# An mLSTM and SoLU kernel: the first product in float16 parts, x turned by a transfer, and a fixed order of operations

## The chip, the cores and the metric

The kernel runs on one core of one Trainium2 chip. The metric is the device time of one execution in microseconds; the value before is the median of 3 runs. The core has a matrix engine (TensorE, PE in the profile; its weight loads are listed as PEld), VectorE (DVE), ScalarE (ACT), GpSimd (POOL) and SyncE (SP), whose queue issues the transfers here. Tiles lie in SBUF; the results of matrix products lie in PSUM, where the kernel keeps eight banks of 128 x 512 float32 values.

## The reference

4 batches, 8 heads, 768 steps, head size 40. For each batch and head a recurrence with gates runs over the steps; its outputs, gated and laid side by side (8 x 40 = 320), are the rows x of a block with d_ff = 1024.

```
for t in range(768):                       # attention part, per batch and head
    m_new  = max(f[t] + m, i[t])
    f_stab = exp(f[t] + m - m_new);  i_stab = exp(i[t] - m_new);  m = m_new
    C = f_stab * C + i_stab * outer(v[t], k[t])
    n = f_stab * n + i_stab * k[t]
    y[t] = sigmoid(o[t]) * (C @ q[t]) / max(abs(n . q[t]), 1)

h    = x @ w_in                            # 3072 x 320 by 320 x 1024
sm   = exp(h - max(h)) / (sum(exp(h - max(h))) + 1e-9)
solu = h * sm
ln   = (solu - mean(solu)) / sqrt(var(solu) + 1e-6) * g_ln
out  = ln @ w_out                          # 3072 x 1024 by 1024 x 320
```

w_in and w_out come as 64-bit floats; the kernel decodes them from their bits.

## The kernel before, in words

**Units.** The steps are cut into 6 chunks of 128, and a unit is one chunk of one batch with all 8 heads: 24 units, chunk by chunk over the batches. For a unit, `unit(u)` sets down these operations.

*Attention.* Transfers on SP's queue bring v and k (`tk`), q and k turned (`qk`), the running gate sums spread over all partitions (`gb`) and, for four units at a time, the output gates (`sg`). ACT makes the decay factors `d` (L990, 8 exponentials of 128 x 128). PE makes the scores `ps` (L1034, into two banks), DVE multiplies them with `d` into `p` (L1047). PE adds up y in a third bank: the inter step `yx` (L1074, old state times q, only for chunks after the first) and two intra steps `yi` (L1101, p times v). DVE normalises (L1117 to L1136), POOL applies the output gate (L1148): that is x. The state step `sx` (L1159) gives this chunk's part of the state, which DVE adds to the decayed state (L1186, or L1188 for the first chunk).

*First product.* PE turns x (L1200, three transposes into a bank), ACT rounds it to the parts `xh` (L1206, L1205) and DVE takes the rest `xl` (L1211, L1217), both in the format float32r. w_in is split alike, as soon as each of its five pieces has been decoded (L675 to L710, then L748 to L777). Of the four part products three are formed: 8 terms, each in two halves of 512 columns, so 16 matmuls a unit (L1245) into one of two double banks `ph`.

*The rest.* DVE takes the row maximum (L1260), ACT the exponential (L1267), DVE h times it (L1282), ACT the squares (L1292) and a float16 rounding (L1306), POOL its remainder (L1310). A transposing transfer turns both float16 parts (L1319). The second product is 24 float16 matmuls of 320 columns (L1378) into the single bank `so_`, ACT scales the result out (L1394, with a factor that POOL's power, L1357, gives) and SP stores it.

**Banks.** `sy` is a ring of three banks for scores, y, the state step's result and the turned x; `ph` has two double banks, `so_` one.

**The order.** Each engine executes its instructions in the order in which they stand, and that order is written out before the program is built. `Plan.find` plays through all operations with the durations and priorities given in the code (`RANK`, `NUDGE`) and lists them in the order of their planned starts; `Plan.run` emits them in this list's order. PE operations with a `mix` number are split into steps (four products, or six matmuls of the second product), and an attention step that is ready together with a step of the first or second product is joined to it: their matmuls are emitted in turn. While PE would be idle at the start, `find` puts in idle matmuls (L1413; each is two passes, 51 of them here), whose results nobody reads. The w_out scale uses L822. Only these few matmuls read float32 in two passes: the attention products, L822 and L1413. The select matrix L498 copies one broadcast column with two operations of a POOL instruction.

## Time and profile before

| | |
|---|---|
| median of 3 runs | 317.56 us (316.15 to 318.75) |
| the profiled execution | 317.33 us, of which its span 315.6 us |
| granted TensorE clock | 0.998 |
| busy: PE, PEld, DVE, ACT, POOL | 297.6, 252.4, 209.4, 202.0, 154.7 us |
| transfers on SP's queue | 59.13 MB, 70.5% of 16 engines' span |

A row of the groups names the line, the engine, the operation, the tiles out<-in and the shape, then `xcount | busy us, mean ns of one | idle us of the engine just before them, and what ended most of it`. A row of the waits reads: engine and line, what it waited for, microseconds in total, times, longest. A row of the chain in order of time has start, duration and what ran; the chain follows back from the last instruction to what released each step, so on PE a piece's duration is what it moved the chain by, not how long the matmul was in the array. A row of the stretches has the stretch, its length, the busy time (and number) of PE, PEld, DVE, ACT and POOL, the clock, the share of the transfer engines and GB/s. In the transfers' row the last number is the median time from issue to landing in us.

### The profile page before, as it was taken

The page shows a single profiled execution, that of the slowest core. Times are in us where ns is not written, and L with a number is a line of the kernel's source. Part 1 is how long each engine was busy: PE and PEld are TensorE (multiplying, and loading weights), DVE is VectorE, ACT ScalarE, POOL GpSimd, SP SyncE. Part 2 cuts the span into 40 slices and gives each one's busy share as a digit, 9 for nine tenths or more (in the row PEclk, how much of TensorE's full clock was granted, in tenths as well). Part 3 has the DMA queues.
Part 4 walks back from the last instruction along what each step waited for, and adds up shares of the span by engine and source line. Part 5 has one row for each costly group of instructions (what it writes and reads, how often), then busy time and mean ns, then how long its engine had stood idle before and what let it go on. Part 6 is the DMA issues. An engine that isn't in the chain of part 4 may idle for free.

```text
span 315.6 us, 6358 instructions
## 1 busy us (share of the span) xinstructions
PE 297.6 (94%) x2255; PEld 252.4 (80%) x2255; DVE 209.4 (66%) x548; ACT 202.0 (64%) x433; POOL 154.7 (49%) x159
## 2 busy tenths in 40 slices
PE   0499999999999999999999999999999999999984
PEld 0398978889778888898889888888988888788753
DVE  5965958999857375766868477764675666574530
ACT  2367669698776866786847678744894754452441
POOL 7165276686685536673672544756334504431300
PEclk9999999999999999999999999999999999999999
DMA  7799937955499955997499754999675534244351
GB/s 230 260 329 393 391 110 247 223 205 86 127 230 247 295 180 82 329 218 226 137 206 281 201 162 115 258 255 259 189 197 150 132 72 58 53 93 84 71 125 43
DMA packets 70255, 59.53 MB, mean 189 GB/s; under 512 B 52944, under 2 KB 59280, under 8 KB 70224
## 3 DMA queue, kind: packets, MB, share of 16 engines
q1 hardware_dynamic: 70224, 59.13, 70.5%
q8 instruction: 18, 0.29, 0.4%
q14 instruction: 13, 0.11, 0.1%
HBM read 42.50 MB, written 4.03 MB: 147 GB/s over the span
## 4 chain that ended last, share of the span: by engine, by line
PE 93%; DVE 4%; issue 1%; DMA 1%; ACT 1%; SPq 0%; ACTq 0%; DVEq 0%
PE ph L1245 31%; PE sy L1101 10%; PE sy L1034 8%; PE sy L1159 5%; PE sy L1074 5%; PE so__163 L1413 4%; PE sy L1200 3%; PE so__404 L822 2%; PE so__1923 L1378 1%; PE so__3758 L1378 1%; PE so__3786 L1378 1%; PE so__3713 L1378 1%; PE so__1761 L1378 1%; PE so__1521 L1378 1%; PE so__2638 L1378 1%
## 5 line engine op out<-in xcount | busy, mean ns | idle before, releaser
L1378 PEld LDWEIGHTS <-big 128*128 128x128 f16 x576 | 62.1, 114 | 17.6 <-issue 5.0
L1101 PEld LDWEIGHTS sy<-tk,p 128*128 128x128 f32 x384 | 63.5, 191 | 6.0 <-DVE p L1047 0.6
L990 ACT ACTIVATE d<-gb,bG 128x128 f32<-128x128 f32 x192 | 60.5, 392 | 6.7 <-DVE p L1047 3.1
L1310 POOL TENSOR_TENSOR us<-e,us 128x1024 f16<-128x1024 f32 x23 | 49.2, 2140 | 29.2 <-ACT us L1306 22.6
L1101 PE MATMUL sy<-tk,p 128*128 128x41 f32 x384 | 56.8, 245 | 0.4 <-DVE p L1047 0.4
L1267 ACT ACTIVATE e<-ph,nm 128x1024 f32<-128x1024 f32 x24 | 26.7, 1112 | 28.0 <-DVE nm L1260 27.8
L1047 DVE TENSOR_TENSOR p<-sy,d 128x512 f32<-128x512 f32 x48 | 31.2, 684 | 18.7 <-PE sy L1034 11.7
L1260 DVE TENSOR_REDUCE nm<-ph 128x1 f32<-128x1024 f32 x24 | 29.3, 1222 | 17.3 <-PE ph L1245 17.1
L1245 PE MATMUL ph<-wih,xh 128*128 128x512 f32 x96 | 40.0, 464 | 0.0
L1148 POOL TENSOR_TENSOR x<-x,sg 128x320 f32<-128x320 f32 x24 | 21.3, 887 | 33.7 <-DVE x L1136 23.0
L1245 PE MATMUL ph<-wil,xh 128*128 128x512 f32 x96 | 37.1, 435 | 0.0
L1282 DVE SCALAR_TENSOR_TENSOR e<-ph,s,e 128x1024 f32<-128x1024 f32 x24 | 30.6, 1276 | 4.0 <-ACT e L1267 3.2
L975 POOL TENSOR_SCALAR_AFFINE_SELECT gb<-gb 128x1024 f32<-128x1024 f32 x24 | 27.1, 1130 | 11.1 <-DMA gb<-gd 11.1
L1292 ACT ACTIVATE sq<-e,a 128x1024 bf16<-128x1024 f32 x24 | 27.6, 1149 | 5.3 <-DVE e L1282 4.4
L1245 PE MATMUL ph<-wih,xl 128*128 128x512 f32 x96 | 30.6, 419 | 0.0
L1034 PEld LDWEIGHTS sy<-qk 40*128 40x128 f32 x384 | 24.1, 193 | 8.0 <-issue 7.5
L1074 PEld LDWEIGHTS sy<-C,qk 128*128 128x128 f32 x160 | 27.4, 191 | 1.9
L1034 PE MATMUL sy<-qk 40*128 40x128 f32 x384 | 28.8, 291 | 0.0
L1306 ACT CAST us<-e 128x1024 f16<-128x1024 f32 x24 | 24.8, 1039 | 3.8 <-DVE e L1282 3.6
L1074 PE MATMUL sy<-C,qk 128*128 128x82 f32 x160 | 27.2, 256 | 0.0
L1159 PEld LDWEIGHTS sy<-tk,kt 128*128 128x128 f32 x160 | 24.9, 191 | 1.3 <-DVE p L1047 0.2
L1159 PE MATMUL sy<-tk,kt 128*128 128x82 f32 x160 | 25.4, 260 | 0.0
(179 smaller groups left out, 594.6 us busy)
## 6 DMA issues: line engine op xcount, KB each, us to landing
qk<-in_qkT_dram SPq DMA_DIRECT2D x24, 512.0 KB, 4.4
gb<-gd SPq DMA_DIRECT2D x24, 512.0 KB, 5.1
tk<-in_tok_dram SPq DMA_DIRECT2D x24, 324.0 KB, 3.5
sg<-in_og_dram SPq DMA_DIRECT2D x12, 320.0 KB, 6.0
out_dram<-ot SPq DMA_DIRECT2D x24, 160.0 KB, 1.8
big<-in_w_out_dram SPq DMA_DIRECT2D x4, 640.0 KB, 11.2
big<-in_w_in_dram SPq DMA_DIRECT2D x4, 512.0 KB, 7.0
big<-in_w_in_dram SPq DMA_DIRECT2D x2, 256.0 KB, 6.2
```

Of the source, the lines that this page charges most:

```text
L990: nc.scalar.activation(out=P[d_t][:, j, n, :], in_=P[gb][:, h, :], func=AF.Exp, bias=P[BG][:, 0, c, b * H + h : b * H + h + 1],)
L1034: nc.tensor.matmul(P[ps[j]][:, n * L : (n + 1) * L], lhsT=P[qk][r, 1, n, :], rhs=P[qk][r, 0, n, :], start=True, stop=True,)
L1047: lambda P, j=j: V.tensor_tensor(out=P[p_t][:, j], in0=P[ps[j]].rearrange("p (n l) -> p n l", l=L), in1=P[d_t][:, j], op=ALU.mult,),
L1074: nc.tensor.matmul(P[yk][:, n * 2 * E1 : (n + 1) * 2 * E1], lhsT=P[qk][:, 0, n, :], rhs=P[old][:, n, :], start=first_of_bank(), stop=False ...
L1101: nc.tensor.matmul(yv(P)[:, h, :], lhsT=P[p_t][:, j, n, :], rhs=v1(P)[:, h, :], start=first_of_bank(), stop=True, skip_group_check=True,)
L1159: nc.tensor.matmul(P[pu][:, n * 2 * E1 : (n + 1) * 2 * E1], lhsT=P[kt][:, 2 * n : 2 * n + 2, :].rearrange("p a d -> p (a d)"), rhs=P[tk][: ...
L1245: nc.tensor.matmul(P[ph][:, j * 512 : (j + 1) * 512], lhsT=a, rhs=w[:, j * 512 : (j + 1) * 512], start=n == 0, stop=n == 7,)
L1260: lambda P: V.tensor_reduce(out=P[nm], in_=P[ph], axis=AX.X, op=ALU.max, negate=True),
L1282: lambda P: V.scalar_tensor_tensor(out=P[e], in0=P[ph], scalar=P[s], in1=P[e], op0=ALU.mult, op1=ALU.mult, accum_out=P[a]),
L1292: lambda P: nc.scalar.activation(out=P[sq], in_=P[e], func=AF.Square, bias=P[a], scale=-float(DFF), accum_out=P[su]),
L1310: lambda P: (V if last else nc.gpsimd).tensor_tensor(out=P[us][:, 1], in0=P[e], in1=P[us][:, 0], op=ALU.subtract),
L1378: nc.tensor.matmul(P[po][:, 0:DM], lhsT=uTv(P, a)[:, k, :], rhs=P[w][:, k, :], start=n == 0, stop=n == 23)
```

## The change

- **Formats.** w_in and x are split into float16 parts instead of float32r. For that w_in gets one scale, a power of two from the largest magnitude of all its five pieces, so each piece is reduced on DVE when it lands (`wabs`), the maximum goes through PE twice (`scale_w_in`), and only then are the pieces decoded, with the scale folded into the first ACT copy. x gets a scale per row from the sum of its magnitudes (ACT, `xm`; DVE, `row_scale` and `hs`). The scales are taken out in the exponential and in the factor of L1282 (`nh`, `s2`: one more tiny DVE operation each).
- **Turning x.** ACT writes the high parts, POOL a scaled copy and the remainders, into one 128 x 640 float16 tile, and a transposing transfer on SP's queue turns it. The three PE transposes, the ACT copies and DVE's subtractions go.
- **Joining.** Steps of the first and of the second product were both joined to attention steps already; the planner now counts different savings for the two. The joins themselves come from the list below.
- **Bank.** The state step's result moves from the `sy` ring to the bank `so_`, in turn with the second product, and x needs no bank, so `sy` serves scores and y alone.
- **Order.** `Plan.run` no longer calls `find` but emits a written list, `ORDER`: operation numbers (in the order in which the code sets them down), a pair for a joined step, and a third number for idle matmuls ahead of it (56 in all).
- **Smaller moves.** q and k are loaded without their 48 padding rows (320 KB instead of 512 KB, in two transfers; the padding is zeroed once by three DVE memsets); output gates come in lots of 4, 8, 8 and 4 units; two tiny DVE operations on the sum z and one on the output factor go to POOL (`z_2`, `row_out`); normalising keeps three small DVE operations; w_in's five loads stand near the head of SP's queue, ahead of the gate stores.

```diff
+ORDER = [
+    24, 22, 4, 5, 25, 291, 29, 7, 147, 23, 31, 0, 33, 35, 8, 37, 3, 9, 2, 6, 195, 32, 27, 10, 26, 243, 1, 15, 11, 125,
...
+    245, 199, 284, 154, 68, 285, 329, 99, 193, 90, (155, 335), 86, 427, 333, 200, 330, 334, 278, 201, 156, 240, 426,
...
+]
...
                 if self.mix[n]:
-                    c = [m for m in avail[eng] if self.mix[m] == 3 - self.mix[n] and ready[m] <= s]
+                    one = self.mix[n] == 1
+                    c = [m for m in avail[eng] if self.mix[m] and (self.mix[m] == 1) != one and ready[m] <= s]
                     if c:
                         m = min(c, key=lambda m: (ops[m][5], m))
                         both.append(m)
-                        ns += ops[m][1] - self.joint[n] - self.joint[m]
+                        ns += ops[m][1] - (self.joint[n][self.mix[m] - 2] if one else self.joint[m][self.mix[n] - 2])
...
-        order, joint, filled = self.find()
...
-    cst("wih", [L, 3, DFF], F32R)
-    cst("wil", [L, 3, DFF], F32R)
+    cst("wih", [L, 3, DFF], F16)
+    cst("wil", [L, 3, DFF], F16)
...
-        load(1750, ld, [raw], prio=RANK[f"sp w_in{i}"][0], behind=[("gb", 0)] if i > 2 else [])
-        decode(raw, HF, wf, lambda P: P[wf][:, 0:HF], prio)
+        load(1750, ld, [raw], prio=RANK[f"sp w_in{i}"][0])
+        P.op(
+            DVE,
+            620,
+            lambda P: V.tensor_reduce(
+                out=P[("wa", 0)][:, i : i + 1],
+                in_=P[raw].rearrange("p (n two) -> p n two", two=2)[:, 0:HF, 1].bitcast(F32),
+                axis=AX.X,
+                op=ALU.max,
+                apply_absolute_value=True,
+            ),
+            [("wa", 0, i)],
+            [raw],
+            prio=RANK["w_abs"][0],
...
+        if i == 4:
+            scale_w_in(RANK["w_abs"][0])
+        parts.append(lambda: split_w_in(i, raw, wf, prio))
+    def scale_w_in(prio):
...
+        wam, wa1, pw = ("wam", 0), ("wa1", 0), ("ph", "wi")
+        P.place[pw] = -1.0
...
+        def one(P):
+            V.tensor_reduce(out=P[wa1], in_=P[pw][0:1, 0:L], axis=AX.X, op=ALU.max)
+            V.tensor_scalar(out=P[wa1], in0=P[wa1], scalar1=2.0**-18, scalar2=None, op0=ALU.max)
+            V.tensor_scalar(
+                out=P[wa1].bitcast(I32), in0=P[wa1].bitcast(I32), scalar1=0x7F800000, scalar2=None, op0=ALU.bitwise_and
+            )
+        P.op(DVE, 480, one, [wa1], [pw], prio=prio)
...
+        def fin(P):
+            V.tensor_copy(out=P[IWI], in_=P[pw][:, L : L + 1])
+            V.tensor_scalar(
+                out=P[WSC].bitcast(I32), in0=P[IWI].bitcast(I32), scalar1=0x7F800000, scalar2=None, op0=ALU.bitwise_xor
+            )
+            V.tensor_scalar(out=P[WSC], in0=P[WSC], scalar1=2.0**-112, scalar2=None, op0=ALU.mult)
+        P.op(DVE, 480, fin, [WSC, IWI], [pw], prio=prio)
...
+    for j in range(QKB):
+        cst(f"qk{j}", [L, 2, NP, L], F32)
+        P.op(DVE, 700, lambda P, j=j: nc.vector.memset(P[(f"qk{j}", 0)], 0.0), [(f"qk{j}", 0)], prio=-200)
...
-    tag("x", [L, DM], F32, 2)
-    tag("xh", [L, 2, L], F32R, 2)
-    tag("xl", [L, 2, L], F32R, 2)
-    tag("x3", [L, L], F32R, 2)
+    tag("x", [L, DM], F32, 3)
+    tag("xs", [L, DM], F32, 2)
+    tag("xq", [L, 2 * DM], F16, 2)
+    tag("xT", [L, 5, L], F16, 4)
...
-        load(1750, lambda P: nc.sync.dma_start(out=P[qk], in_=qkT[b, c]), [qk], prio=rank(SPQ, "qk"), behind=[("gb", u - 2)] if u > 1 else [])
+        def ld_qk(P):
+            for j in range(2):
+                nc.sync.dma_start(out=P[qk][64 * j : 64 * j + D], in_=qkT[b, c, j])
+        load(1150, ld_qk, [qk], prio=rank(SPQ, "qk"), behind=[("gb", u - 2)] if u > 1 else [])
...
+        rd, x = ("rd", u), ("x", u)
+        def norm(P):
+            n = yv(P)[:, :, D]
+            V.tensor_scalar(out=P[rd], in0=n, scalar1=-1.0, scalar2=1.0, op0=ALU.mult, op1=ALU.max)
+            V.tensor_tensor(out=P[rd], in0=n, in1=P[rd], op=ALU.max)
+            V.reciprocal(out=P[rd], in_=P[rd])
+        op(DVE, 520, norm, [rd], y)
...
+        xm, xr, hs, xs, xq, xT = (("xm", u), ("xr", u), ("hs", u), ("xs", u), ("xq", u), ("xT", u))
+        op(
+            ACT,
+            670,
+            lambda P: nc.scalar.activation(out=P[xs], in_=P[x], func=AF.Abs, accum_out=P[xm]),
+            [xm, xs],
+            [x],
+        )
+        def row_scale(P):
+            V.tensor_scalar(out=P[xm], in0=P[xm], scalar1=TINY, scalar2=2.0**-15, op0=ALU.max, op1=ALU.mult)
+            V.reciprocal(out=P[xr], in_=P[xm])
+        op(DVE, 310, row_scale, [xm, xr])
...
-            pu, cn = bank("u", 0.3), (f"C{b}", u)
+            pu, cn = bank("u", 0.3, "so_"), (f"C{b}", u)
...
+        op(
+            ACT,
+            470,
+            lambda P: nc.scalar.activation(out=P[xq][:, 0:DM], in_=P[x], func=AF.Copy, scale=P[xr]),
+            [(*xq, 0)],
+            [x, xr],
+        )
+        op(
+            POOL,
+            700,
+            lambda P: nc.gpsimd.tensor_scalar(out=P[xs], in0=P[x], scalar1=P[xr], scalar2=None, op0=ALU.mult),
+            [xs],
+            [x, xr],
+        )
         def lo_x(P):
-            V.tensor_tensor(
-                out=P[xl],
-                in0=P[px][:, 0 : 2 * L].rearrange("p (k l) -> p k l", k=2),
-                in1=P[xh].bitcast(F32),
-                op=ALU.subtract,
-            )
-            V.tensor_tensor(
-                out=P[x3][KR:L], in0=P[px][0:KR, 2 * L : 3 * L], in1=P[x3][0:KR].bitcast(F32), op=ALU.subtract
-            )
-        op(DVE, 705, lo_x, [xl, (*x3, 1)], [px, xh, (*x3, 0)])
+            for o, n, w in ((DM + KR, 0, 2 * L), (DM, 2 * L, KR)):
+                nc.gpsimd.tensor_tensor(
+                    out=P[xq][:, o : o + w], in0=P[xs][:, n : n + w], in1=P[xq][:, n : n + w], op=ALU.subtract
+                )
+        op(POOL, 1000, lo_x, [(*xq, 1)], [xs, (*xq, 0)])
+        op(
+            SPQ,
+            500,
+            lambda P: nc.sync.dma_start_transpose(out=P[xT], in_=P[xq]),
+            [xT],
+            [(*xq, 0), (*xq, 1)],
+            after=950,
...
+        P.place[ph] = float(u)
+        terms = [(0, WIH, 0), (0, WIL, 0), (1, WIH, 1), (1, WIL, 1), (3, WIH, 0), (4, WIH, 1), (2, WIH, 2), (2, WIL, 2)]
...
+                a, w, k = terms[n]
                 nc.tensor.matmul(
                     P[ph][:, j * 512 : (j + 1) * 512],
-                    lhsT=a,
-                    rhs=w[:, j * 512 : (j + 1) * 512],
+                    lhsT=P[xT][:, a, :],
+                    rhs=P[w][:, k, j * 512 : (j + 1) * 512],
                     start=n == 0,
                     stop=n == 7,
                 )
-            op(PE, 932, Steps(4, first), [ph], first_in[g], mix=2)
-        nm, z, e, mx, s, a, su, sq = (("nm", u), ("z", u), ("e", u), ("mx", u), ("s", u), ("a", u), ("su", u), ("sq", u))
+            op(PE, 868, Steps(4, first), [ph], [xT, *first_in[g]], mix=3)
...
+            lambda P: nc.scalar.activation(
+                out=P[e], in_=P[ph], func=AF.Exp, bias=P[nh], scale=P[hs], accum_out=P[z]
+            ),
             [e, z],
...
+        def z_2(P):
+            nc.gpsimd.tensor_scalar(out=P[z], in0=P[z], scalar1=1.0e-9, scalar2=P[mx], op0=ALU.add, op1=ALU.mult)
+            nc.gpsimd.tensor_scalar(
+                out=P[ab], in0=P[z], scalar1=P[z], scalar2=EPS_Z**2, op0=ALU.mult, op1=ALU.mult
+            )
+        op(POOL, 500, z_2, [z, ab], [mx])
...
+        def row_out(P):
+            nc.gpsimd.tensor_tensor(out=P[pw], in0=P[ab], in1=P[MH], op=ALU.pow)
+            nc.gpsimd.tensor_scalar(out=P[so], in0=P[pw], scalar1=P[OW], scalar2=None, op0=ALU.mult)
+        op(POOL, 800, row_out, [pw, so], [ab, MH, OW])
...
+        P.place[po] = u + 4.5
```

More of the change, by code (lines that the diff above doesn't have):

```diff
@@ L95 @@
[L95 to L111 removed]
[105 rows of a table removed]
[L217 removed]
+    "sp w_in0": (2.9,),
+    "w_abs": (3.66,),
@@ L264, in tag, with op @@
         self.tags[name] = (bufs, make)
-    def op(self, eng, ns, fn, out=(), inp=(), prio=0.0, after=0, busy=1.0, behind=(), mix=0, lock=False, joint=0):
+    def op(self, eng, ns, fn, out=(), inp=(), prio=0.0, after=0, busy=1.0, behind=(), mix=0, lock=False, joint=(0, 0)):
         self.joint[len(self.ops)] = joint
@@ L414, in run @@
         ops = self.ops
-        order, joint, filled = self.find()
+        if ORDER:
+            rows = [(x,) if isinstance(x, int) else x for x in ORDER]
+            order = [n for r in rows for n in r[:2] if n >= 0]
+            joint = {r[0]: r[1] for r in rows if len(r) > 1 and r[1] >= 0}
+            filled = {r[0]: r[2] for r in rows if len(r) > 2}
+        else:
+            order, joint, filled = self.find()
         skip = set(joint.values())
@@ L1081, in inter @@
                 )
-            op(PE, 860, Steps(NP, inter), y, [qk, (*old, 0), (*old, 1)], busy=0.65, mix=1, name="yx", joint=125)
+            op(PE, 860, Steps(NP, inter), y, [qk, (*old, 0), (*old, 1)], busy=0.65, mix=1, name="yx", joint=(125, 140))
             op(
@@ L1165, in upd @@
                 )
-            op(PE, 860, Steps(NP, upd), [pu], [kt, tk], busy=0.65, mix=1, name="sx", joint=125)
+            op(PE, 860, Steps(NP, upd), [pu], [kt, tk], busy=0.65, mix=1, name="sx", joint=(125, 140))
             if c > 0:
@@ L1192, in unit @@
             Ccur[b] = cn
-        px, xh, xl, x3 = (bank("p", 1.25), ("xh", u), ("xl", u), ("x3", u))
-        def tr_x(P):
-            for k in range(3):
-                w = L if k < 2 else KR
-                nc.tensor.transpose(P[px][0:w, k * L : (k + 1) * L], P[x][:, k * L : k * L + w], P[I])
-        op(PE, 500, tr_x, [px], [x, I], name="px")
-        def hi_x(P):
-            nc.scalar.copy(out=P[x3][0:KR], in_=P[px][0:KR, 2 * L : 3 * L])
-            nc.scalar.copy(out=P[xh], in_=P[px][:, 0 : 2 * L].rearrange("p (k l) -> p k l", k=2))
@@ L1410, in idle @@
     def idle(P):
-        if ("so_", "idle") not in P.tiles:
-            P.tiles[("so_", "idle")] = P.tags["so_"][1]()
-        nc.tensor.matmul(P[("so_", "idle")][:, 0:L], lhsT=P[I], rhs=P[I], start=True, stop=True)
-    P.fill = (216, idle, (BG, ("so_", "m")))
+        k = next(k for k in reversed(P.tiles) if k[0] == "so_")
+        nc.tensor.matmul(P[k][:, 384:512], lhsT=P[I], rhs=P[I], start=True, stop=True)
+    P.fill = (216, idle, (BG, ("ph", "wm")))
     with tc.manual_schedule():
```

341 lines of the change are left out of this document (168 added, 173 removed), and 166 rows, old and new, of tables (NUDGE, ORDER).

## The prediction

> **What bounds the kernel now.** I read the page's busy shares and slices first, then PE's waits, then the chain of waits by line.
>
> ```profile
> span 315.6 us, 6358 instructions
> PE 297.6 (94%) x2255; PEld 252.4 (80%) x2255; DVE 209.4 (66%) x548; ACT 202.0 (64%) x433; POOL 154.7 (49%) x159
> PE   0499999999999999999999999999999999999984
> ...
> PE so__137 L599 <- DVE sg L585: 11.0, 1, 11.0
> PE so__163 L1413 <- DVE bG L606: 1.1, 1, 1.1
> PE so__3713 L1378 <- ACT ot L1394: 0.7, 1, 0.7
> ...
> by line: PE ph L1245 31.3%; PE sy L1101 9.9%; PE sy L1034 8.2%; PE sy L1159 4.9%; PE sy L1074 4.8%; PE so__163 L1413 4.0%; PE sy L1200 2.5%; PE so__404 L822 1.5%; issue 1.1%; PE so__1923 L1378 1.1%; PE so__3758 L1378 1.1%; PE so__3713 L1378
> ```
>
> TensorE starts after 11.0 us and from 13.5 us never waits a microsecond again; the longest later wait is 0.7 us, in the tail. The chain lies on PE almost throughout, so what an edit takes from PE's row of work comes off the span, as long as the other engines (66% at most) keep up. But a busy PE may be loading weights rather than streaming. The next look is therefore the chain in order of time, where each piece is what PE advanced by (start, duration, line).
>
> ```profile
> 66.29 1.77 PE sy L1101 x16
> 118.43 1.63 PE so__1361 L1378 x12
> ...
> 102.07 0.33 PE sy L1200 x3
> 104.08 0.15 PE sy L1101 x2
> 104.52 0.27 PE so__1210 L1378 x2
> 105.73 0.31 PE ph L1245
> 106.04 0.15 PE sy L1101 x2
> 106.19 0.30 PE ph L1245
> 107.10 1.95 PE ph L1245 x8
> 109.05 1.09 PE sy L1034 x16
> 111.24 0.18 PE sy L1074 x2
> 111.43 0.27 PE ph L1245
> ```
>
> A float32 attention product is two passes. Alone a pass costs 1.77/16 = 0.111 us (0.222 a product), although it streams only 41 columns: its weight load sets it. Between large matmuls the pair costs 0.15 (intra, L1101) or 0.18 (L1074, and L1159 alike), its first load being hidden. A float16 second-product matmul costs 1.63/12 = 0.136 alone and 0.27/2 = 0.135 in such a neighbourhood. A first-product matmul costs 1.95/8 = 0.24 among its own kind, but 0.30 to 0.31 behind an intra pair and 0.27 behind an inter pair: today what interleaving gives the small product it takes back from the large one, 0.15 + 0.305 being 0.222 + 0.235.
>
> **The change, on PE.** First product in float16: 384 matmuls as before. They take 31.3% of 315.6 = 98.8 us of chain, 0.257 each. The nearest float16 row is L1378's, 320 columns in 0.136; by columns 512 take 0.217, and since that row shows no surcharge behind small products I charge none: 384 x 0.217 = 83.3, **-15.5 us**. Bounds: the old 0.235 throughout would be 90.2, so 8.6 of the gain is the surcharge and 6.9 the columns; if neither moved, 0.
>
> The Trainium skill, "TensorE: Matmul & The Clock Gate", Part 3, The mechanism, says that a weight load overlaps a running matmul only when the row groups differ. All these tiles fill 128 rows, so by it the loads would stay in the open and the -15.5 would be the columns' -6.9. The 0.135 beside the intra pairs speaks against it.
>
> Transposes: L1200's 72 matmuls go, 2.5% = **-7.9 us** (0.33/3 = 0.11 each, in agreement).
>
> Attention products: the new ORDER list names what runs joined. Counted in it: of 48 intra steps (four products each) 24 join a first-product step, 12 a second-product step, 12 run alone: 36x4x0.149 + 12x4x0.222 = 32.1, against 9.9% = 31.2 now, **+0.9**. Of 40 inter and state steps 35 are joined: 35x4x0.183 + 5x4x0.222 = 30.1, against 9.7% = 30.6, **-0.5**. So the interleaving adds hardly anything by count; its gain is the surcharge above. Scores (1.09 a unit) and the second product stay. PE in all: **-23.0 us**.
>
> **The head.** w_in now needs one scale over all five pieces before any is decoded, and the list puts more attention ahead of the first product.
>
> ```profile
> 39.95 0.87 PE L1245 MATMUL ph<-wih,xh 128*128 128x512 f32 x2
> ...
> 9.92 0.94 DVE L585 TENSOR_TENSOR sg<-sg 32x768 f32<-32x768 f32 x1
> ...
> L683 DVE TENSOR_SCALAR e<-us 128x512 int32<-128x512 int32 x5 | 2.1, 414 | 0.0
> L699 DVE SCALAR_TENSOR_TENSOR e<-big,e 128x512 int32<-128x512 int32 x5 | 3.4, 687 | 0.1
> L710 DVE SCALAR_TENSOR_TENSOR e<-big,e 128x512 int32<-128x512 int32 x5 | 4.8, 967 | 0.1
> L1047 DVE TENSOR_TENSOR p<-sy,d 128x512 f32<-128x512 f32 x48 | 31.2, 684 | 18.7 <-PE sy L1034 11.7 <-ACT d L990 6.7
> L1132 DVE RECIPROCAL rd<-rd 128x8 f32<-128x8 f32 x24 | 4.8, 199 | 0.5
> L1136 DVE TENSOR_TENSOR x<-sy,rd 128x320 f32<-128x320 f32 x24 | 11.7, 489 | 0.7
> L1186 DVE TENSOR_TENSOR C<-C,sy 64x164 f32<-64x164 f32 x32 | 10.3, 322 | 5.6 <-PE sy L1159 4.9
> L1260 DVE TENSOR_REDUCE nm<-ph 128x1 f32<-128x1024 f32 x24 | 29.3, 1222 | 17.3 <-PE ph L1245 17.1
> ...
> L675 ACT ACTIVATE us<-big 128x512 f32<-128x512 f32 (+1 forms) x9 | 6.5, 720 | 9.5 <-DMA big<-in_w_in_dram 8.0 <-DMA big<-in_w_out_dram 1.4
> ```
>
> DVE is in-order, and I follow its list. The gate work of L585 ends at 10.9. Two of the five new reductions stand ahead of that (half of L1260's width, 0.61 each): 12.1. Three more and a small one: 14.1. The gate copy, some seven tiny operations and two trips through PE for the scale: about 16.4, my estimate. ACT's first scaled copy 0.7: 17.1. Then three pieces are decoded, 3 x (0.41 + 0.69 + 0.97) = 6.2, with some 1.6 of waits and small work: 24.9. From there to the last mask of unit 3 the list has 33 DVE operations: eight masks 5.5, decoding of w_in's rest 4.1 and of w_out 4.7 (its 640 columns in proportion), three units' normalising 3.1 (L1136 and three of L1132's kind), four state adds 1.3, small ones 1.3: 20.0, and 1.6 between them. That is 46.5; one intra step and unit 4's score follow on PE, so the first product starts near **48**, 8 us after today's 39.95. PE uses the delay: ahead of its first product the list has 5 scores, 8 intra and 3 state steps (5x1.09 + 11x0.89 = 15.2 us), the trace today 10.1 (2 scores, 4 intra, 2 state steps, 3 transposes, 8 passes of L822). So 8.1 - 5.1 = **+3.0 us**; bounds 0 (attention not held by DVE) and 6 (w_in's loads, now ahead of the gate stores on SP's queue, later by 3). The three memsets for q and k lie in DVE's idle time before the gates land.
>
> **Off the path.** x now goes through ACT (a sum of magnitudes, a scaled cast), DVE (two tiny operations), POOL (a scaled copy, two subtractions) and a transposing transfer on SP's queue. That is some 10 us instead of 3, but in the list PE has between a unit's last intra step and its first-product step at least 13.4 us of work by the prices above (28 in the middle): hidden.
>
> ```profile
> L1310 POOL TENSOR_TENSOR us<-e,us 128x1024 f16<-128x1024 f32 x23 | 49.2, 2140 | 29.2 <-ACT us L1306 22.6 <-issue 6.6
> L1148 POOL TENSOR_TENSOR x<-x,sg 128x320 f32<-128x320 f32 x24 | 21.3, 887 | 33.7 <-DVE x L1136 23.0 <-DVE z L1334 8.8 <-ACT sg L1003 0.9
> L498 POOL TENSOR_SCALAR sel<-ident 128x128 f32<-128x128 f32 x1 | 1.0, 972 | 0.0
> L1357 POOL TENSOR_TENSOR pw<-ab,mhalf 128x1 f32<-128x1 f32 x24 | 13.2, 552 | 18.3 <-DVE ab L1350 18.2
> ...
> 312.26 0.53 ACT L1394 ACTIVATE ot<-so__3786,so 128x320 f32<-128x320 f32 x1 [3.56 <-PE so__3786 L1378]
> ...
> big<-us SPq DMA_TRANSPOSE x25, 5.3
> ...
> 100.00:200.00 100.00, 100.00 (x787) 86.72 (x786) 66.84 (x184) 71.73 (x159) 55.77 (x58) 1.00 0.79 206
> ```
>
> POOL (fifth column, 55.8 us of 100; DMA share 0.79) has some 6.2 us a unit (154.7/24, less the start's work) and gains the subtractions (0.9 at L1148's rate), the scaled copy, and three one-column operations (0.1 to 0.55 each, take 0.75 in all). The copy is 0.9 by L1148's rate, 2.4 by L498's; I take 0.9, since L498 read a broadcast column. So 8.9 a unit, at the high end 11.2, against PE's new pace: units 10 to 20 of the list hold 104 us, 10.4 a unit. ACT gains some 0.5 a unit and DVE loses some: both stay under 80%. Transfers lose 192 KB of q and k a unit and gain 160 KB transposed (5/16 of one that lands in 5.3 us now); with the pace up about a tenth the share goes to roughly 0.9. Behind a transpose that waits for POOL on SP's queue stand the next units' loads.
>
> "SBUF — State Buffer", Who interferes with whom, in the Trainium skill, makes GpSimd and VectorE exclude each other while one holds their shared port, which speaks against more POOL work. Over its 23 executions L1310 stays within 2127 to 2158 ns here, so I charge nothing.
>
> **One bank for state and second product.** State product (L1159) and second product now take turns in one bank: 34 hand-overs up to unit 20, each needing an eviction (two L1186 adds, 0.65, or L1394, 0.53) while PE does other work. By the list that work is 1.2 to 2.9 us each time, so they fit unless the evicting engine is inside a long operation; with the tail as now I allow **+1.0**.
>
> **Sum.** 315.6 - 23.0 + 3.0 + 1.0 = 296.6 span. The profiled execution took 317.33, 1.7 more than its span and 0.2 under the median of 317.56; with both the forecast is 298.5, **298**. Its own range is 292 (no loss in the head, no stalls and a little in hand) to 305 (columns at the old rate).
>
> **Rivals.**
> *POOL paces.* The scaled copy costs 2.4: 11.2 against 10.4 a unit, 0.8 x 16 units = 13 us. For it: POOL's only row of that kind; against: POOL idles 44% of the middle. 311, chance 0.12.
> *The float16 loads are not hidden behind the short intra passes.* L1245's surcharge of 8.6 stays: 298 + 8.6 = 307, chance 0.06. For it: every such load shows the surcharge in float32 today; against: L1378's show none. That is what the rule on row groups would make of it.
> *The head is later still*, SP's w_in loads holding gates and q and k: PE waits 6 us more, 304, chance 0.06.
> *The one bank serialises.* The eviction stands behind a 1.2 us reduction or exponential, PE's in-order row behind the bank. The gain of 19 us is gone at 19/34 = 0.57 us a hand-over; at 1.0 us each it is 34 us: **332**, slower. For it: today's back-to-back hand-overs cost 0.7 (L1394's row); against: 1.2 us or more of other work stand between them. Chance 0.08.
> The forecast has 0.68.
>
> A measurement here can tell about 1% from no change. Faster by more than that (under 314.4): 0.68 + 0.06 + 0.06 + half of POOL's case = 0.86; within 1%: 0.06, the other half; slower: 0.08. The range 289 to 310 leaves out the bank and most of POOL's case; its low end is the forecast's own with the pair prices 1% too high.
>
> **What would show it.** L1245's share of chain near 83 us, its matmuls 0.22 apart both alone and behind intra pairs; no L1200; the first product near 48 us; POOL's scaled copy under 1 us; no PE wait on DVE's state adds or ACT's L1394 longer than a microsecond before the tail. It is wrong if PE's row in the slices falls below 9 in the middle, or if its waits name POOL, a transpose or the bank's evictions for more than 5 us.

## The result and the profile after

The changed kernel takes **306.26 us** (median of 4 runs, 304.77 to 309.68) against 317.57 for the kernel before on the same chip: a ratio of 0.963, 95% interval 0.957 to 0.969. A second set of runs of the same kernel gave 308.80, ratio 0.970 (0.965 to 0.976). So it is faster, by 9 to 12 us where the prediction had 19. Its profiled execution took 309.68 us, 1.8 more than its span. It counts as a slow one, and the ratios here and below leave out such executions (those over 1.5% above the fastest of their kernel): the other three of the first set took 304.77 to 306.74.

The page of the changed kernel: span, busy shares, PE's row of the 40 slices and the granted clock, then PE's waits.

```profile
span 307.9 us, 6421 instructions
PE 282.8 (92%) x2196; PEld 224.4 (73%) x2196; DVE 209.7 (68%) x566; ACT 208.9 (68%) x451; POOL 225.6 (73%) x303
PE   0179989999899999999999999999999999999984
PEclk9999979999999999999999999999999999999999
```

```profile
PE so__137 L571 <- DVE sg L556: 12.4, 1, 12.4
PE ph L755 <- DVE wam L750: 2.8, 1, 2.8
PE sy L1138 <- DVE mx L1353: 1.2, 1, 1.2
PE sy L1165 <- DVE p L1111: 1.2, 1, 1.2
PE so__3870 L1442 <- ACT ot L1458: 0.8, 1, 0.8
...
PE so__471 L1480 <- DVE C L1263: 0.3, 1, 0.3
```

PE's row is at 9 from the seventh slice on up to the tail, but for the eleventh (77 to 85 us), which has 8: PE waits 1.2 us there for a small DVE operation (L1353). By the letter of the prediction's sign (a slice below 9 in the middle) that one counts against it. Nearly all the other holes ahead of the tail are in the first 53 us. No wait names POOL; one of 0.5 us, at 157 us, names the transposing transfer (xT), and none before the tail names the shared bank for more than 0.3 us. In this execution the granted clock fell to 0.79 between 40 and 48 us, as in some of the runs below and not in others, which makes it some 1.6 us longer than without.

Lines have moved: the first product is L1314 now (L1245 before), the second L1442, the intra steps L1165, the scores L1098, inter and state steps L1138 and L1234, the idle matmuls L1480. The first product in the chain in order of time, behind state steps, behind intra steps and in line with its own kind:

```profile
101.02 0.22 PE ph L1314
101.23 0.18 PE so__1134 L1234 x2
...
103.41 0.86 PE ph L1314 x4
...
126.25 0.15 PE sy L1165 x2
126.40 0.22 PE ph L1314
126.62 0.15 PE sy L1165 x2
126.77 0.22 PE ph L1314
```

It moves the chain by 0.22 nearly everywhere, where before it took 0.24 among its own kind and 0.31 behind an intra pair. From the end of one matmul to the end of the next, over the whole trace, it takes 0.216 behind its own kind (167 times), 0.217 behind an intra pair (92) and 0.216 behind inter and state pairs (105), and 0.32 only the seven times that it follows scores. The pair costs 0.15 and 0.18, as before.

The other engines in the middle (same columns as before), and POOL's new work:

```profile
100.00:200.00 100.00, 99.49 (x827) 81.17 (x825) 64.95 (x197) 72.84 (x168) 86.75 (x119) 1.00 0.96 203
L1280 POOL TENSOR_SCALAR xs<-x,xr 128x320 f32<-128x320 f32 x24 | 27.9, 1164 | 4.5 <-DVE xr L1217 2.7 <-DVE mx L1353 1.7
L1287 POOL TENSOR_TENSOR xq<-xs,xq 128x256 f16<-128x256 f32 (+1 forms) x48 | 23.0, 501 | 2.4 <-ACT xq L1273 1.1 <-POOL x L1201 0.6 <-POOL C L1247 0.2
L1390 POOL TENSOR_TENSOR us<-e,us 128x1024 f16<-128x1024 f32 x23 | 49.1, 2135 | 3.9 <-ACT us L1386 3.7
```

POOL is busy for 86.75 of 100 us (8.9 of 10.4 a unit was forecast, 86%), the transfers' share is 0.96, and PE still has 99.5.

Now the two halves of the span. The first product starts here:

```profile
57.21 0.39 PE L1314 MATMUL ph<-wih,xT 128*128 128x512 f16 x1
```

From there to the end the span is 307.9 - 57.2 = 250.7 us; the forecast was 296.6 - 48 = 248.6, and before it was 315.6 - 39.95 = 275.6. What the prediction says of everything behind the first product came out within 2 us. The start did not: 57.2 in place of 48, **9.2 us of the 11.3** by which the span exceeds its forecast. The chain of waits in the head shows what lies there:

```profile
15.44 6.89 DMA qk<-in_qkT_dram
...
22.38 2.81 PE sy L1098 x16
25.19 4.65 PE so__137 L1480 x22
...
43.15 4.45 PE so__345 L1480 x24
47.59 1.73 PE sy L1165 x16
...
51.59 1.62 PE so__471 L1480 x12
...
54.44 1.75 PE sy L1165 x16
56.19 1.09 PE sy L1098 x16
```

Idle matmuls are on the chain for more than ten of these 35 us: the 22 passes of one block take 4.65, 0.21 each, where 12 passes later take 1.62. The first scores take 2.81 and the last ones 1.09. PE runs at half its later speed here. The 1.00 that the page gives for the granted clock ahead of 29 us is no reading: this trace's clock records begin at 29.33 us, with full speed, and the views count a stretch without a record as 1.00. The dip is on record: half speed for 3.41 us, from 42.99 to 46.40 us (0.79 is the mean over the 8 us), and it is what makes the second block slow. The stretch below has the clock third from the end.

```profile
43.00:46.00 3.00, 3.00 (x17) 2.92 (x14) 2.58 (x6) 2.90 (x9) 1.67 (x3) 0.50 0.57 183
```

DVE's side of it: the waits of DVE between 26 and 54 us, and its busy time in that stretch (third pair of numbers).

```profile
DVE rd L1181 <- PE sy L1165: 3.9, 2, 3.6
DVE p L1111 <- PE sy L1098: 1.9, 1, 1.9
26.00:54.00 28.00, 26.25 (x216) 25.04 (x216) 20.95 (x45) 21.05 (x48) 17.46 (x18) 0.94 0.94 276
```

DVE works 20.95 us, where the prediction's list had 20.0, and stands still for 7.05, where it had 1.6. It waits for PE, which is at its idle matmuls and at the attention steps behind them.

### The profile page after: what moved, and what is told of

It reads as the page before. It is cut to its first block, busy times and chain, and to the rows that moved or that the text cites. A ratio compares the mean times of both kernels' runs of the same rounds, so it can differ in the third digit from the quotient of the medians.

```text
span 307.9 us, 6421 instructions
## 1 busy us (share of the span) xinstructions
PE 282.8 (92%) x2196; PEld 224.4 (73%) x2196; DVE 209.7 (68%) x566; ACT 208.9 (68%) x451; POOL 225.6 (73%) x303
## 4 chain that ended last, share of the span: by engine, by line
PE 78%; DVE 9%; DMA 5%; issue 4%; ACT 2%; POOL 1%; SPq 0%; DVEq 0%; ACTq 0%; POOLq 0%
PE ph L1314 24%; PE sy L1165 10%; PE sy L1098 8%; PE sy L1138 5%; DMA qk<-in_qkT_dram 2%; DMA xT<-xq 2%; PE so__137 L1480 2%; PE ph L874 2%; PE so__345 L1480 1%; DMA gd<-sg 1%; PE so__3959 L1442 1%; PE so__1786 L1442 1%; PE so__2103 L1442 1%; PE so__3180 L1442 1%; PE so__2676 L1442 1%
## 5 line engine op out<-in xcount | busy, mean ns | idle before, releaser
L1314 PE MATMUL ph<-wih,xT 128*128 128x512 f16 x240 | 78.0, 382 | 0.5 <-DMA xT<-xq 0.5
L1442 PEld LDWEIGHTS <-big 128*128 128x128 f16 x576 | 59.4, 107 | 22.8 <-issue 2.8
L1165 PEld LDWEIGHTS sy<-tk,p 128*128 128x128 f32 x384 | 58.3, 193 | 6.4 <-DVE p L1111 1.8
L1314 PEld LDWEIGHTS <-xT 128*128 128x128 f16 x384 | 47.4, 127 | 18.0 <-DMA xT<-xq 0.8
L1165 PE MATMUL sy<-tk,p 128*128 128x41 f32 x384 | 56.2, 249 | 1.2 <-DVE p L1111 1.2
L1390 POOL TENSOR_TENSOR us<-e,us 128x1024 f16<-128x1024 f32 x23 | 49.1, 2135 | 3.9 <-ACT us L1386 3.7
L1314 PE MATMUL ph<-wil,xT 128*128 128x512 f16 x144 | 48.9, 381 | 0.0
L1039 POOL TENSOR_SCALAR_AFFINE_SELECT gb<-gb 128x1024 f32<-128x1024 f32 x24 | 26.7, 1111 | 22.7 <-DMA gb<-gd 22.4
L1111 DVE TENSOR_TENSOR p<-sy,d 128x512 f32<-128x512 f32 x48 | 32.1, 682 | 7.6 <-PE sy L1098 6.0
L1330 DVE TENSOR_REDUCE nm<-ph 128x1 f32<-128x1024 f32 x24 | 29.2, 1217 | 11.6 <-PE ph L1314 11.5
L1344 ACT ACTIVATE e<-ph,nh,hs 128x1024 f32<-128x1024 f32 x24 | 28.7, 1196 | 10.2 <-DVE nh L1337 10.2
L1280 POOL TENSOR_SCALAR xs<-x,xr 128x320 f32<-128x320 f32 x24 | 27.9, 1164 | 4.5 <-DVE xr L1217 2.7
L1138 PEld LDWEIGHTS sy<-C,qk 128*128 128x128 f32 x160 | 27.8, 190 | 4.0 <-issue 1.6
L1098 PE MATMUL sy<-qk 40*128 40x128 f32 x384 | 29.6, 291 | 0.6 <-DMA qk<-in_qkT_dram 0.6
L1201 POOL TENSOR_TENSOR x<-x,sg 128x320 f32<-128x320 f32 x24 | 21.2, 883 | 11.6 <-DVE x L1189 8.5
L1098 PEld LDWEIGHTS sy<-qk 40*128 40x128 f32 x384 | 24.6, 193 | 6.8 <-issue 3.9
L1138 PE MATMUL sy<-C,qk 128*128 128x82 f32 x160 | 27.0, 256 | 1.2 <-DVE mx L1353 1.2
L1287 POOL TENSOR_TENSOR xq<-xs,xq 128x256 f16<-128x256 f32 (+1 forms) x48 | 23.0, 501 | 2.4 <-ACT xq L1273 1.1
```

Of the source, the lines that this page charges most:

```text
L1098: nc.tensor.matmul(P[ps[j]][:, n * L : (n + 1) * L], lhsT=P[qk][r, 1, n, :], rhs=P[qk][r, 0, n, :], start=True, stop=True,)
L1111: lambda P, j=j: V.tensor_tensor(out=P[p_t][:, j], in0=P[ps[j]].rearrange("p (n l) -> p n l", l=L), in1=P[d_t][:, j], op=ALU.mult,),
L1138: nc.tensor.matmul(P[yk][:, n * 2 * E1 : (n + 1) * 2 * E1], lhsT=P[qk][:, 0, n, :], rhs=P[old][:, n, :], start=first_of_bank(), stop=False ...
L1165: nc.tensor.matmul(yv(P)[:, h, :], lhsT=P[p_t][:, j, n, :], rhs=v1(P)[:, h, :], start=first_of_bank(), stop=True, skip_group_check=True,)
L1280: lambda P: nc.gpsimd.tensor_scalar(out=P[xs], in0=P[x], scalar1=P[xr], scalar2=None, op0=ALU.mult),
L1314: nc.tensor.matmul(P[ph][:, j * 512 : (j + 1) * 512], lhsT=P[xT][:, a, :], rhs=P[w][:, k, j * 512 : (j + 1) * 512], start=n == 0, stop=n == 7,
```

## The experiments

All in one table; "first product" is where it starts in the profiled execution of the run, "records from" where the clock records of its trace begin (in every run PE's passes get twice as fast there), "dip" where they show half speed in the first 60 us of the span. The medians are of all executions of a run.

| run | edit | first product, us | records from, us | dip, us | median, us | ratio to before (95%) |
|---|---|---|---|---|---|---|
| after_again | none | 57.5 | 28.6 | 42.2 to 45.6, 55.9 to 59.3 | 308.80 | 0.970 (0.965 to 0.976) |
| a4_unjoined | first product apart, changed kernel | 55.4 | 29.4 | none | 313.96 | 0.983 (0.979 to 0.986) |
| b1_before_unjoined | first product apart, kernel before | 40.7 | 21.2 | none | 317.27 | 0.999 (0.997 to 1.002) |
| a1_no_idle | no idle matmuls | 59.3 | 63.2 | none | 313.85 | 0.987 (0.982 to 0.991) |
| h1_half_idle | half of them | 56.6 | 48.2 | none | 309.02 | 0.972 (0.966 to 0.979) |
| d1_f16_idle | four 16-bit ones for each | 57.1 | 29.5 | 43.1 to 46.5 | 309.99 | 0.977 (0.972 to 0.982) |
| a2_qk_first | unit 0's loads first | 54.4 | 29.3 | none | 308.41 | 0.970 (0.963 to 0.976) |
| a3_no_abs | maximum known | 57.4 | 30.1 | 43.7 to 47.2 | 306.88 | 0.967 (0.961 to 0.973) |
| c3_both | both | 52.5 | 23.6 | 30.5 to 33.9 | 307.48 | 0.968 (0.962 to 0.974) |
| e1_light_decode | w_out's decoding cut | 55.4 | 31.1 | none | 305.92 | 0.963 (0.958 to 0.969) |
| w1_keep_warm | more idle matmuls, in PE's gaps | 55.7 | 20.0 | 54.2 to 57.6 | 308.48 | 0.969 (0.966 to 0.973) |
| w2_masks_first | that, and masks earlier on DVE | 59.6 | 21.9 | 35.6 to 45.8 | 311.75 | 0.980 (0.977 to 0.983) |

a4_unjoined changes nothing ahead of the first product, so its 55.4 is also the changed kernel's head without the dip; 57.2 to 57.5 is that head with it. (The heads differ a little otherwise: in a4_unjoined q and k landed 1.3 us later and the first slow block was 0.5 us shorter.)

### Is the gain the surcharge of the small products?

a4_unjoined and b1_before_unjoined emit the joined steps of the first product one behind the other, in the changed kernel and in the kernel before:

```diff
+        joint = {a: c for a, c in joint.items() if "ph" not in (ops[a][3][0][0], ops[c][3][0][0])}
         skip = set(joint.values())
```

> The changed kernel with the first product's steps emitted beside the attention steps that the list joins to them, not in turn with them: 24 intra steps and 28 inter and state steps of four products each. By the pair prices (an intra product 0.149 joined and 0.222 alone, an inter or state product 0.183 and 0.224, the float16 first-product matmul 0.216 in both): 96 x 0.073 + 112 x 0.041 = 11.6 us more, 318 us. Rival (another engine paces the middle, POOL with 73% or the transfers with 79%): PE has room, under 5 us more.

> The kernel before with its float32r first product emitted beside the attention steps that it is joined to, not in turn with them; the joins with the second product stay. By the pair prices the joins bring nothing there (0.15 + 0.305 joined, 0.222 + 0.235 apart, and apart the first load of a step still hides): 315 to 318 us, no change. Rival (the joins were worth something before too): 3 to 6 us slower, as without joins in the changed kernel.

Measured: the kernel before doesn't care (317.27, ten runs, against 317.51). The changed kernel's ratio goes from 0.963 in the first set and 0.970 in the second to 0.983, a loss of 4 to 6 us. In the traces its time from the first product to PE's last matmul goes from 247.3 to 253.9, +6.6. The chain of a4_unjoined about the same place, steps apart:

```profile
107.22 1.09 PE sy L1099 x16
108.31 1.05 PE so__1287 L1235 x8
109.36 2.59 PE ph L1315 x12
111.95 0.85 PE sy L1139 x8
...
125.24 0.82 PE sy L1166 x8
```

The matmul costs 2.59/12 = 0.216 alone as well, so what joining saves is on the side of the small products: a state or inter step of eight passes mostly takes 0.85 alone (1.05 right behind scores) and 4 x 0.183 = 0.73 in turn, an intra step 0.82 alone and 4 x 0.15 = 0.60 in turn. For the 28 and 24 joined steps that is 28 x 0.12 + 24 x 0.22 = 8.6 us; a4_unjoined doesn't have the two waits of the changed kernel's PE behind the first product (1.2 and 0.5), which leaves 6.9 for the measured 6.6. In float32r the large matmul took that back, within the 1 us or so of the interval; in float16 it doesn't. That is the prediction's 8.6 us of surcharge, by this measurement some 4 to 7. (The forecast for this run, 11.6, was too high since it took 0.222 and 0.224 a product alone, where these rows have 0.82/4 = 0.205 and 0.85/4 = 0.21, and since it left out the waits.)

### What holds the head?

**The idle matmuls.** a1_no_idle has none:

```diff
-... (138, -1, 11), ... (183, -1, 3), ... (146, -1, 9), ... (235, -1, 12), ...
+... 138, ... 183, ... 146, ... 235, ...
```

> The changed kernel without the 56 idle matmuls that its list puts into the head; nothing else is altered. Theory A (the missing 8 us lie in the head, and the written blocks of idle matmuls are part of it): with PE not yet at full clock a pass takes about 0.2 us (22 passes in 4.72 us from 25.1), and a block ends after the mask that it bridges is ready (first mask of unit 0 done at 27.0, its intra step at 29.7; first mask done of unit 2 at 43.9, its intra step at 47.4). Without them the first product comes 4 to 6 us earlier: 301 to 303 us. Rival B (clock): the blocks keep PE warm; without them attention's passes in the head take twice as long and nothing is won, or 1 to 3 us are lost: 306 to 309.

The idle matmuls gone, PE is slower, not faster. Its chain, late in the head:

```profile
44.67 3.64 PE sy L1164 x16
...
50.09 2.01 PE sy L1097 x16
...
59.38 1.82 PE ph L1313 x4
```

Sixteen intra passes take 3.64 (1.73 above), scores 2.01 (1.09), the first four first-product matmuls 1.82 (0.97). From 41 us on PE is busy almost without a break (8.00 of 8 us from 48 to 56), and it stays at half speed until the first product has begun, for about 20 us; the trace's clock records begin at 63.2 us. So the idle matmuls are needed, and 313.85 is above the theory's 301 to 303 and the rival's 306 to 309.

d1_f16_idle has four bfloat16 matmuls (one pass each) for each idle matmul:

```diff
-... (138, -1, 11), ...
+... (138, -1, 44), ...
-        nc.tensor.matmul(..., lhsT=P[I], rhs=P[I], start=True, stop=True)
+        nc.tensor.matmul(..., lhsT=P[IDB], rhs=P[IDB], start=True, stop=True)
```

> The changed kernel with each idle matmul (float32, two passes of 128 columns with slow weight loads) replaced by four bfloat16 ones of 128 columns, so that PE streams instead of loading weights in the same time. Theory D (PE's speed in the head follows how much it streams; float32 passes alone left it at half speed for 20 us in the run without idle matmuls): full speed some 4 us after the first long block, near 23 us instead of 30, blocks and attention steps after it at half the time, first product 3 to 5 us earlier: 301 to 303 us. Theory A (DVE's list sets the head): PE waits for masks instead, no more than 1 us gained.

Half speed until about 30 us just the same, and 309.99: what the idle matmuls are made of made no difference to that.

h1_half_idle halves the numbers, rounded down:

```diff
-... (138, -1, 11), ... (183, -1, 3), ... (146, -1, 9), ... (235, -1, 12), ...
+... (138, -1, 5), ... (183, -1, 1), ... (146, -1, 4), ... (235, -1, 6), ...
```

> The changed kernel with each block of idle matmuls cut to half (25 in place of 56); nothing else differs. In its trace the two longest blocks end 4.65 and 4.45 us after they begin, while DVE waits 1.9 and 3.6 us for what PE has queued behind them. Theory 'the blocks stand in PE's row': they end about half as late, the first product starts 3 to 5 us earlier (about 53 in place of 57) and the time is 302 to 304. Rival 'PE's speed': without the filling PE stays slow for longer, as it did with none of them (scores 2.0 us in place of 1.09, first product at 59.3); then the first product starts at 57 to 59 and the time is 306 to 312.

The blocks are half as long in number, but now PE stays slow up to 48 us:

```profile
42.58 2.01 PE sy L1098 x16
44.59 2.86 PE so__328 L1480 x12
...
55.61 1.09 PE sy L1098 x16
```

Twelve passes take 2.86, as long as 24 at full speed. First product 56.6 against 55.4, and 309.02: the rival holds, a little ahead of its 57 to 59.

**The loads and the maximum.** a2_qk_first issues unit 0's loads ahead of w_in's (first diff). a3_no_abs puts the known maximum in place of the five reductions (second). c3_both does that too and issues unit 0's loads right behind w_in's (third).

```diff
-    24, 22, 4, 5, 25, 291, 29, ... 37, 3, ... 125, ... 126, ...
+    4, 5, 23, 125, 126, 24, 22, 25, 291, 29, ... 37, 3, ...
```

```diff
-            lambda P: V.tensor_reduce(out=P[("wa", 0)][:, i : i + 1], ...),
+            lambda P: V.memset(P[("wa", 0)][:, i : i + 1], 1.636129...),
```

```diff
-... 37, 3, 9, ... 11, 125, ... 41, 126, ...
+... 37, 125, 126, 3, 9, ... 11, ... 41, ...
```

> The changed kernel with unit 0's v, k and q, k loads (and the one memset that the latter need) ahead of the five loads of w_in on SP's queue. Rival C (the chain of waits read at its word: the load of q and k, 6.9 us on the chain, holds the first score at 22.4): the first score and all behind it come 4 to 6 us earlier, 301 us. Theory A: the score is not what is late, since the first mask stands behind the decoding of three pieces of w_in on DVE (it ran at 26.3); w_in lands about 2 us later, so 306 to 308 us.

> The changed kernel with the five reductions over w_in (0.67 us each on DVE) replaced by tiny memsets to the largest magnitude known beforehand: it leaves out finding the maximum, so the scale no longer waits for all five loads. Theory A: the scale, ready at 18.9 in the changed kernel, comes about 3 us earlier, decoding starts at the loads' pace, and as DVE's list sets the head the total falls by 3 to 5 us: 301 to 303. Rival B' (PE with its idle matmuls sets the head by itself): under 1 us.

> The changed kernel with both late inputs of the head made early: the largest magnitude of w_in known beforehand (it leaves out finding it), and unit 0's v, k, q and k loaded directly behind w_in's loads and ahead of the gate stores. Theory A' (scale and first score were level, so that each alone gained nothing): the first mask on DVE, at 26.3 before, comes some 4 us earlier and so does the first product: 301 to 303 us. Theory D (PE itself sets the head, its idle matmuls and attention passes running at half speed up to about 30 us): under 2 us, 304 to 307.

> The changed kernel itself, beside the other three on the same chip: 305 to 307 us, first product at 54 to 57 us, and about 247 us from there to PE's last matmul, as in the kernels of the first four runs that keep the joins (247.2 to 247.5).

Neither alone moves the time: 308.41 and 306.88 against 306.26 and 308.80. With the loads first, q and k no longer hold the scores, but w_in's largest magnitude does, and the first scores start at 23.9 instead of 22.4; the first product is 1.0 earlier than a4_unjoined's. This trace shows most plainly what sets the head: from the first scores to the first product PE is busy for 30.14 of 30.54 us and waits for nobody, DVE for 26.32 (PE, PEld, DVE, ACT, POOL as before):

```profile
23.86:54.40 30.54, 30.14 (x270) 28.74 (x269) 26.32 (x61) 28.19 (x68) 21.73 (x21) 1.00 1.01 294
```

With the maximum known, the scores wait for q and k as before. Both together bring the first scores to 18.2 and the first product to 52.5 in the profiled execution, although PE waits 1.7 us for a mask there and a dip of 3.41 us follows (30.5 to 33.9 us); that execution took 305.19. The other three took 307.22 to 309.29, with a mean granted clock of 0.976 to 0.983 where the profiled one had 0.994, so they lost more to the clock. What the two together are worth is not settled: executions of one kernel lie up to 5 us apart.

**DVE's list.** e1_light_decode:

```diff
-                out=di(P), in0=lw(P), scalar=29, in1=di(P), ...
+                out=cut(di(P)), in0=cut(lw(P)), scalar=29, in1=cut(di(P)), ...
```

> The changed kernel with the decoding of w_out cut: of its three DVE operations a piece, the second and third treat one column only in place of 640, so w_out's values lack their sign and their low bits (the rest of the work is as before). Up to unit 3's last mask that takes some 3.6 us from DVE's list (1.78 + 0.81 + 0.97 + 0.81 in the trace, less 0.2 each). Theory 'DVE's list sets the head', as the prediction had it: the first product starts 3 to 4 us earlier (about 53.5) and the time is 302 to 304. Rival 'PE's row sets it' (idle matmuls and half speed): DVE only waits longer, the first product moves by less than 1 us, and the time stays at 306 to 309.

First product at 55.4, as in a4_unjoined; 305.92 against 306.26 and 308.80. (That it is the same to the tenth is partly luck: the first scores start 0.7 us earlier than in a4_unjoined, and the slow passes behind them take 1.1 us more.) The two largest of DVE's waits between 26 and 54 us:

```profile
DVE p L1114 <- PE sy L1101: 3.4, 3, 2.5
DVE rd L1184 <- PE sy L1168: 2.8, 3, 2.0
```

DVE still waits for PE, and PE waits for DVE only once there, for 0.2 us. The prediction's premise, that DVE's list sets the start of the first product, doesn't hold here: less work on DVE only lengthens its waits.

**PE without gaps.** w1_keep_warm and w2_masks_first:

```diff
-... (42, -1, 1), ... 47, 135, ... (187, -1, 9), ...
+... (42, -1, 7), ... 47, (135, -1, 2), ... (187, -1, 13), ...
```

```diff
-... 53, 48, ... 44, ... 136, ... 21, 180, (138, -1, 11), 64, 137, 62, 133, (183, -1, 3), 70, 65, ...
+... 53, 136, 137, 21, 48, ... 44, ... 180, (138, -1, 5), 64, 62, 133, (183, -1, 3), 184, 70, 65, 185, ...
```

> The changed kernel with idle matmuls added where its trace shows PE waiting in the head: 6 more while the largest magnitude of w_in is found (13.9 to 16.7 us), 2 ahead of the first scores (21.8 to 22.4), 4 more ahead of an intra step of unit 1 (39.8 to 41.0). Nothing else differs. Theory 'gaps keep PE slow': without them the idle passes are at 0.11 us from some 24 us on in place of 29.7, the slow stretch at 43 to 47.4 is gone, the first product starts at 52 to 54 and the time is 302 to 304.5. Rival 'the speed of the head is not set by such gaps': the slow passes last to about 30 us as before, the added matmuls stand in PE's row, the first product starts at 57 to 58.5 and the time is 306 to 310.

> As the run before it in its first two blocks of idle matmuls, and with unit 0's two masks put ahead of the last operations of w_in's decoding on DVE, unit 1's masks ahead of the decoding of the last two pieces, and the longest block behind the first scores cut from 11 to 5. Unit 0's mask then starts near 24.5 us in place of 26.3, and PE's row has 1.3 us less in it. Theory 'order of DVE and length of the blocks set the head beside PE's speed': the first product starts another 2 to 3 us earlier than in the run before it, and the time is 300 to 303. Rival 'PE's speed alone': no earlier than that run, 304 to 309.

w1_keep_warm gets its speed and not its gain. PE by time, with the wait ahead of each in brackets:

```profile
17.00 3.25 PE L1480 MATMUL so__137<-ident 128*128 128x128 f32 x14
20.49 1.38 PE L1480 MATMUL so__137<-ident 128*128 128x128 f32 x10
...
25.07 2.72 PE L1480 MATMUL so__137<-ident 128*128 128x128 f32 x22
28.95 1.09 PE L1165 MATMUL sy<-tk,p 128*128 128x41 f32 x8 [1.16 <-DVE p L1111]
```

From 20.5 us on PE is at full speed, nine microseconds earlier than in the changed kernel. But the added block stands ahead of the matmul that spreads w_in's maximum, so the scale, the decoding and the first mask come 1.9 us later (28.2 in place of 26.3), and now it is DVE that PE waits for. A dip of the clock (half speed from 54.2 to 57.6 us) slows the last scores. From the first mask to the first product it is 55.7 - 28.2 = 27.5, against 30.9.

w2_masks_first moves the masks, and gains 3 us up to unit 0's last intra step (29.3 in place of 32.4 us). Then:

```profile
PE so__348 L1234 <- POOL kt L1080: 4.8, 1, 4.8
POOL gb L1039 <- DMA gb<-gd: 2.4, 1, 2.4
```

The state step waits for POOL's weighted keys, POOL stands in order at the next unit's gate sums, and these wait for a transfer of 512 KB. PE is still, its clock goes to half from 35.6 to 45.8 us, and the first product comes at 59.6. So the head has several bounds close together: PE's row, DVE's list, POOL's row behind a transfer, the transfers of q and k and of w_in. Taking one away gives 0 to 3 us here before the next one holds. None of these kernels beats the changed one clearly.

Not tried: a head in which all four are moved at once, and the planner's own order in place of the written list.

## Why the prediction was right and wrong

- **First product, -15.5: right.** The matmul was costed at 0.217 everywhere and measured 0.216 alone, behind intra and behind state pairs: 384 x 0.216 = 82.9 against 83.3. From end to end of PE's matmuls, the few behind scores with it, it takes 83.9 us in all, and the kernel before 98.8. (Its share of the chain, 24.4% of 307.9 = 75.1 us, is no measure of that any more: the chain lies on PE for 78% of the span now, 93% before.) The trace decides against the sentence of the Trainium skill, "TensorE: Matmul & The Clock Gate", Part 3, The mechanism, by which a load overlaps a running matmul only when the row groups differ, so that these full-row loads could not be hidden. Both kernels' weight loads show a difference: about 0.19 us each in float32r, 0.098 in float16, in the rows below (shortest, median and longest in ns, of one stretch; over the whole span the float16 ones have a median of 0.138 and a mean of 0.127). The Trainium skill, "TensorE: Matmul & The Clock Gate", Weight-path perf modes, says that a faster weight load is used for 128 weights of a type other than float32; no run here switches it, but the shorter load agrees.

```profile
L1314 PEld LDWEIGHTS <-xT x14: 95/98/138, 57.2 to 61.9; 128*128 128x128 f16 x14
```

```profile
L1245 PEld LDWEIGHTS ph<-wih,xh x12: 187/190/193, 39.9 to 59.9; 128*128 128x128 f32 x12
```

- **Transposes, -7.9: right; the attention pairs, +0.9 and -0.5: prices right, sums a little low.** No PE transposes of x are left, and the pairs keep 0.15 and 0.18. From end to end, the intra steps take 32.7 us (31.2 before) and the inter and state steps 31.5 (30.5): +1.5 and +1.0.
- **Bank and stalls, +1.0: a little low.** Behind the first product the span has 2.1 us more than forecast. PE's waits there add up to some 4 us (1.2 for L1353, 0.5 for xT and the tail's 2.3), against 2.0 before: 2 more where 1.0 was allowed. No hand-over of the bank is among them until the tail, so the one bank doesn't serialise.
- **POOL: the copy was mis-sized, without effect.** 1.16 us against 0.9 (the prediction's sign was under 1), it is nearer to the row it was costed by (0.9) than to the high end (2.4). The parts of the forecast's 8.9 a unit add up to 8.75; and with the copy at 2.4 alone they give 10.25, below PE's 10.4, since the rival's 11.2 also has the three small operations at their high end. POOL's load of 86.75 in 100 is what was forecast, and PE kept 99.5: POOL doesn't pace. L1390's mean stays too (2135 ns, 2140 before), as charged.
- **The head, +3.0 with bounds 0 to 6: the step that failed.** Against the forecast 48 the first product came at 57.2 in the profiled execution (55.4 without the dip). Reckoned as in the forecast, the head costs 57.2 - 39.95 - 5.1 = 12.2 us (10.4 without the dip), outside its bounds. First mask at 26.3 for 24.9: +1.4. From it to the end of unit 3's last mask (52.73 + 0.68 = 53.4) 27.1 for 21.6: +5.5, and that is not DVE's work (20.95 for 20.0) but its waits (7.05 for 1.6). From there to the first product 3.8 for 1.5: +2.3, a state step, two intra steps and the scores that were still queued on PE. The list was followed on one engine; PE was taken to have room, because only its attention work was counted (15.2 us). The 56 idle matmuls, 112 passes of 0.11 and more, were in the front matter and in no sum. Counted from the first scores they are 100 passes, 11.2 us at full speed, and PE's row then ends where it was found: 22.4 + 5 x 1.1 scores + 7.3 intra + 3.3 state + 11.2 = 49.7, plus half speed (2.81 for 1.1 and 4.65 for 2.4 in the first two pieces, 4.0) and the second slow block (4.45 for 2.88, 1.6, the dip) = 55.3; waits and short gaps make up the rest. The run that leaves DVE less to do (e1_light_decode) and the one in which PE doesn't wait at all (a2_qk_first) bear that out.
- **"The head is later still": right in size, wrong in cause.** It had 304 by w_in's loads holding gates, q and k. Loading q and k first (a2_qk_first) gave nothing in the time.

The forecast's 298 therefore misses mainly by the head: 8 us by the first set's median, 11 by the second's. That the range held it is luck: its upper bound was set for other reasons, and no term of the sum had idle matmuls or half speed in it.

## What to carry to other kernels

Where an order is written out, follow it on every engine, fillers included, before one of them is called the bound; a filler block is work like any other for the operation behind it, and at the start it took up to twice its later time here. Compare the durations of like pieces before believing a granted clock of 1.00, which here also stood for no record. What joining a small matmul to a large one saves depended here on the large one's format (float16 or float32r; that its shorter weight load is the reason fits, but no run separates the two): measure the pair on both sides, in the formats that will be used. And a start-up stretch in which several engines and transfers run nearly level won't shrink by taking one of them away.

## What was not expected of the hardware

- PE's half speed in the head, where the views show a granted clock of 1.00. It ended at 29.3 us in the changed kernel, at 20.0 in w1_keep_warm, at 48.2 in h1_half_idle, and at 63.2, with the first product begun, in a1_no_idle; these are the times at which the clock records of the traces begin. In h1_half_idle PE was slow though nearly always busy (stretch, length, PE's busy time first, then PEld, DVE, ACT, POOL, clock; the 1.00 stands for no record):

```profile
24.00:32.00 8.00, 8.00 (x46) 7.33 (x43) 6.07 (x14) 6.90 (x12) 4.28 (x4) 1.00 0.99 318
```

The Trainium skill, "TensorE: Matmul & The Clock Gate", Part 1, What's actually happening, has the array warm after one busy window of about 3.4 us. w1_keep_warm agrees (slow from 16.5 to 20.0 us); h1_half_idle and a1_no_idle, slow for some 20 us and more of float32 attention passes, don't. In every trace full speed came within some 3 us of 128-column idle matmuls or of the first product, or up to 1 us behind, and never among attention passes alone; no run isolates what decides, and it stays open.

- The dips. Each in these heads is half speed for 3.41 us, or for three times that in w2_masks_first. The dip at 42 to 44 us isn't chance alone: it is there in the four traces in which PE had just waited 1.0 to 1.5 us for a mask (after, after_again, a3_no_abs, d1_f16_idle), and not in the three in which it waited 0.5 us or less (a4_unjoined, e1_light_decode, a2_qk_first). But the one in w1_keep_warm and the second one in after_again come behind attention steps without such a wait, and no run isolates the cause.

- One of the decoding's three DVE operations is longer than in the kernel before at the same width: L654 takes 0.60 us on average at 512 columns, up to 0.74, where 0.41 was costed. The other two take 0.68 and 0.73 (0.69 and 0.97 before), so the three together are as long as they were, and the cause wasn't tested.
